# GpSimd's splits cut into tiles, a new order at the end of the activation, and routing sums as accumulating products

## The chip, the cores and the metric

The kernel runs on one core of one Trainium2 chip. The metric is the device time of the whole kernel in microseconds (us), as the median of several executions. TensorE does the matrix products (PE in the profile; PEld is its load of the stationary operand), VectorE (DVE), ScalarE (ACT) and GpSimd (POOL) the elementwise work, and SyncE (SP) issues the DMA transfers. SBUF is the on-chip memory, PSUM the accumulators that TensorE writes.

## What is computed

Linear attention by random features, a dense layer with the mish activation, and a mixture of experts with one expert per token, cut from the reference:

```python
# q, k, v: 2 x 8 heads x 576 x 64; omega: 128 x 64
def phi(x):
    proj = einsum('bhsd,md->bhsm', x, omega); sq = sum(x*x)/2
    h = proj - sq
    return exp(h - max(h)) / sqrt(m)
kv = einsum('bhsm,bhsd->bhmd', phi(k), v); z = sum(phi(k), axis=2)
x = num / den            # num = phi(q) kv,  den = phi(q) z + 1e-6
...
h = x @ w_in             # 1152 tokens x 512 -> 2048
g = h * tanh(softplus(h))
y = g @ w_out            # 2048 -> 512
...
logits = y @ w_gate      # 8 experts
e = argmax(logits); gate = softmax(logits)[e]
# in token order: a token is kept while its expert has fewer than `capacity` (288) tokens
out = gate * (relu(y @ w1[e]) @ w2[e])   # 0 for tokens that are not kept
```

## The kernel before

**Precision.** Large operands are float32 and are split into a high part in fp32r (a rounded copy) and a low part (what the rounding left): `split_hi_lo`, one cast (L56 on ScalarE, L58 on GpSimd, L60 on VectorE) and one subtraction (L62, on VectorE or GpSimd). Each product is then three matmuls (L66, L67, L68), so every operand is split before TensorE can start on it. `w_in` and `w_out` arrive as words that VectorE first turns into float32, in three instructions to a chunk (L109, L111, L113).

**Attention (0 to about 80 us).** The 16 heads are taken in 8 pairs `p`, in a loop over `i`; a pass of it has five beats, each with one `proj` on TensorE (`pj`), one `phi` (the maximum on VectorE, the exponential on ScalarE, for some halves after a subtraction on VectorE, L235), and extra work for earlier pairs: transposes (`qtr`, result `qT`), sums over keys (`kvm`), `den` and `num` (L282). The operand `kqf` of a pair (1024 columns for an even one, 1280 for an odd one) is loaded two or three passes ahead, by a DMA on SyncE's queue whose buffer must have been released by an earlier split, and split into `kqh` and `kql`: by ScalarE and VectorE for pair 0, ScalarE and GpSimd for pair 1, and GpSimd alone for pairs 2 to 7, in one cast and one subtraction for the whole pair, issued before the first beat of a pass. `num` ends with a split of its own result `x` (576 columns) into `xh` and `xl` on GpSimd. VectorE converts the first chunks of `w_in` in between. The order of each engine's instructions in this stage is the order of the code.

**h (about 80 to 200 us).** For 16 blocks `j` of the hidden layer and 3 groups `c` of tokens, `hmm(j,c)` is a product of `x` and `w_in`, and `hout` copies it to `g` (L422). `mish` turns `g` into the activation in steps: "s" (sigmoid) and "l" (logarithm) on ScalarE, "t" a tanh on ScalarE (L470) and a product on VectorE (L471). ScalarE has to load a table (`table`) between kinds of function. `wturn` and `wgate_u`/`wgate_s` work out w_out · w_gate, so that the logits (`lg`, L477) come from `g` itself; `wgate_s` waits for a copy `us` of `wgate_u`'s result (L441).

**First pass over w_out (about 202 to 245 us).** `ymm(ps0,j)` adds block `j` of `g` times `w_out` for a first group of 288 tokens; `prep(j)` splits `w_out`'s block (`wl`, `whi`) and `g`'s (`gh`) ahead of it. Between the 16 products stand the last logits and the routing: `route0` (argmax, as a one-hot `oh`), `route1` (each token's place among the tokens of its expert, `rp`), `route2` (counts, and which expert's tokens take the next steps). From here on everything is an order written by hand. Then come a second pass for a group of tokens that the routing chose, two experts, and a rest that is skipped when no token is left.

In `route1`, a token's place is the sum over earlier tokens in its tile (a product with `ub`, a triangle of ones) and over all earlier tiles: the latter from `cu`, a running sum of the one-hots over the 12 tiles of 96 tokens, made in `route0` by copies and additions on VectorE (L660 to L666):

```python
T.matmul(out=p[:TT, 0:96], lhsT=ub, rhs=fl(R["ohb"]), start=True, stop=False)
T.matmul(out=p[:TT, 0:96], lhsT=onesb, rhs=fl(R["cu"]), start=False, stop=True)
```

Of the kernel before, what the change touches and what calls it, by code (L numbers as in the profile page):

```python
# [32 lines left out]
def performer_mish_moe(  # L33
# [132 lines left out]
    with ExitStack() as c2:  # L166
# [136 lines left out]
        def num(u, k, last=False):  # L303
# [13 lines left out]
            split_hi_lo(x, xh[:, e + k, c], xl[:, e + k, c], *(("act", "dve") if last else ("pool", "pool")))  # L317
# [98 lines left out]
    with tc.manual_schedule():  # L416
# [19 lines left out]
        def wgate_u(b):  # L436
# [4 lines left out]
            S.copy(out=us[b], in_=u)  # L441
# [37 lines left out]
        chunk, ghl = {}, {}  # L479

# [31 lines left out]
        for j in range(NJ):  # L512
# [20 lines left out]
            for c in range(3):  # L533
                if (j, c) not in h_early:
                    hout(j, c, hmm(j, c))
                if c == 0:
# [27 lines left out]
                if c == 1:  # L564
# [3 lines left out]
                    if j == 15:  # L568
                        prep(1, slice(0, GT), "dve", "pool")
# [14 lines left out]
        prep(2, slice(0, GT), "dve", "pool")  # L584
# [22 lines left out]
        def route0(lgs):  # L607
# [25 lines left out]
            V.tensor_scalar(out=cand, in0=pv, scalar1=0.0, scalar2=-1000.0, op0=ALU.is_ge, op1=ALU.mult)  # L633
            yield
            V.tensor_tensor(out=cand, in0=cand, in1=iota, op=ALU.add)
            yield
# [12 lines left out]
            V.tensor_reduce(out=sm, in_=ex, op=ALU.add, axis=AX.X)
# [6 lines left out]
            R["gate"] = gate  # L656
            cu = [small(f"cu{i}", sh, BF16) for i in range(2)]
            V.memset(cu[0][:, 0:1, :], 0.0)
            yield
            V.tensor_copy(out=cu[0][:, 1:, :], in_=ohb[:, 0 : NTT - 1, :])  # L660
            yield
            k, a = 1, 0
            while k < NTT:
                V.tensor_copy(out=cu[1 - a][:, 0:k, :], in_=cu[a][:, 0:k, :])
                yield
                V.tensor_tensor(out=cu[1 - a][:, k:, :], in0=cu[a][:, k:, :], in1=cu[a][:, : NTT - k, :], op=ALU.add)  # L666
                yield
                k, a = 2 * k, 1 - a
            R["ohb"], R["cu"] = ohb, cu[a]

        def route1():
            fl = lambda a: a.rearrange("p t e -> p (t e)")
            sh = [TT, NTT, E]
            p = bank("qt", "rp")
            T.matmul(out=p[:TT, 0:96], lhsT=ub, rhs=fl(R["ohb"]), start=True, stop=False)
# [324 lines left out]
```

## Time and profile before

| | |
|---|---|
| time, median of 3 runs | 333.21 us (332.83 to 333.98) |
| the profiled execution | 333.5 us, of it 331.7 us the span that the trace covers |
| mean granted clock of TensorE | 0.975 |
| busy, share of the span | PE 93%, PEld 84%, DVE 67%, ACT 61%, POOL 26% |
| the chain that ended last | PE 73%, DVE 11%, ACT 7%, DMA 4% |

The span is from the first to the last instruction on the trace; the rest of the profiled time lies around it. The granted clock is TensorE's share of full speed. The busy share is an average over stages: what a change in one of them is worth has to be read from that stage's own waits.

### The profile page before, as it was taken

To read this page: it belongs to the slowest core of one execution; us is meant where nothing else is said; L and a number is where in the kernel's file an instruction comes from. 1 tells how busy PE (TensorE), PEld (TensorE's weight loads), DVE (VectorE), ACT (ScalarE), POOL (GpSimd) and SP (SyncE) were. 2 spreads that over 40 slices of the span, in tenths; PEclk is the share of its full clock that TensorE was granted. 3 is DMA by queue.
4 is the path that set the end of the run, shared out by engine and by line. 5 is a ranking of instruction groups with operands and counts; after the bars stand their busy time and mean duration, and the time that the engine had idled before them with its cause. 6 is when DMAs were issued, how large, how long until landed. Compare 5 with 4: busy or idle time off the path is not lost.

```text
span 331.7 us, 5881 instructions
## 1 busy us (share of the span) xinstructions
PE 307.7 (93%) x2223; PEld 279.4 (84%) x2224; DVE 221.6 (67%) x405; ACT 201.2 (61%) x383; POOL 85.1 (26%) x65
## 2 busy tenths in 40 slices
PE   8978988999999999999999998499599999999992
PEld 5966865877999899889988995489599999999991
DVE  5769897763798696977778489498564465314411
ACT  5955674765149978878797795745244672506311
POOL 2884682213000000000000013477401460332300
PEclk9997997999999999999999999899799999999998
DMA  7796532000066339926160000000034545441011
GB/s 216 248 322 204 176 104 87 28 0 2 0 204 241 128 127 300 278 89 218 38 251 2 0 2 0 0 4 1 2 109 138 166 127 191 158 131 54 21 36 41
DMA packets 18065, 36.88 MB, mean 111 GB/s; under 512 B 1552, under 2 KB 7376, under 8 KB 18032
## 3 DMA queue, kind: packets, MB, share of 16 engines
q1 hardware_dynamic: 18032, 36.45, 33.7%
q8 instruction: 19, 0.31, 0.4%
q14 instruction: 14, 0.11, 0.1%
HBM read 32.91 MB, written 3.54 MB: 110 GB/s over the span
## 4 chain that ended last, share of the span: by engine, by line
PE 73%; DVE 11%; ACT 7%; DMA 4%; issue 2%; SPq 1%; POOL 1%; ACTq 0%; POOLq 0%; DVEq 0%
PE h L66 9%; PE h L67 9%; PE h L68 9%; PE py L66 7%; PE py L67 7%; PE py L68 7%; PE kvp L249 3%; PE num L282 3%; PE ph L66 2%; PE ph L67 2%; PE ph L68 2%; DMA wi<-w_in 2%; DVE wif L113 2%; PE lg L477 2%; PE wt L433 2%
## 5 line engine op out<-in xcount | busy, mean ns | idle before, releaser
L62 POOL TENSOR_TENSOR wl<-wl,whi 128x512 fp32r<-128x512 f32 x32 | 44.2, 1384 | 191.6 <-DVE whi L60 131.1
L66 PE MATMUL h<-xh,wih 128*128 128x384 f32 x192 | 66.5, 346 | 0.5 <-DVE g L422 0.5
L68 PE MATMUL h<-xh,wil 128*128 128x384 f32 x192 | 64.4, 336 | 0.0
L67 PE MATMUL h<-xl,wih 128*128 128x384 f32 x192 | 64.4, 336 | 0.0
L66 PE MATMUL py<-gh,whi 128*128 128x288 f32 x128 | 39.8, 311 | 1.3 <-DVE g L422 1.3
L66 PEld LDWEIGHTS h<-xh,wih 128*128 128x128 f32 x192 | 36.1, 188 | 5.0 <-issue 2.9
L68 PE MATMUL py<-gh,wl 128*128 128x288 f32 x128 | 39.2, 307 | 0.0
L67 PE MATMUL py<-gh,whi 128*128 128x288 f32 x128 | 39.1, 305 | 0.0
L67 PEld LDWEIGHTS h<-xl,wih 128*128 128x128 f32 x192 | 36.1, 188 | 0.5 <-issue 0.5
L68 PEld LDWEIGHTS h<-xh,wil 128*128 128x128 f32 x192 | 36.0, 188 | 0.0
L471 DVE TENSOR_TENSOR g<-g,em 128x1152 f32<-128x1152 f32 x16 | 22.7, 1426 | 13.9 <-ACT em L470 13.9
L230 DVE TENSOR_REDUCE nm<-pj 128x4 f32<-128x512 f32 x36 | 24.3, 686 | 11.4 <-PE pj L68 11.2
L237 ACT ACTIVATE e<-pj,nm 128x128 f32<-128x128 f32 x72 | 22.4, 382 | 15.3 <-DVE e L235 8.5
L66 PEld LDWEIGHTS py<-gh,whi 128*128 128x128 f32 x128 | 25.4, 199 | 6.7 <-issue 3.7
L62 DVE TENSOR_TENSOR gh<-g,gh 128x288 fp32r<-128x288 f32 x32 | 21.4, 672 | 12.1 <-ACT gh L56 11.8
L56 ACT CAST gh<-g 128x288 fp32r (+1 forms) x26 | 11.3, 434 | 25.7 <-PE py L68 21.3
L68 PEld LDWEIGHTS py<-gh,wl 128*128 128x128 f32 x128 | 25.4, 199 | 0.0
L67 PEld LDWEIGHTS py<-gh,whi 128*128 128x128 f32 x128 | 25.4, 198 | 0.0
L56 ACT CAST whi<-wl 128x512 fp32r<-128x512 f32 x41 | 24.2, 616 | 1.1 <-PE py L67 1.0
L66 PE MATMUL pj<-omh,kqh 128*128 128x256 f32 x72 | 22.9, 319 | 0.8 <-ACT e L240 0.8
L422 DVE COPY g<-h 128x384 f32<-128x384 f32 x36 | 19.9, 552 | 4.2 <-PE h L68 4.2
L458 ACT ACT_TABLE_LOAD x17 | 21.8, 1283 | 0.3
(156 smaller groups left out, 735.0 us busy)
## 6 DMA issues: line engine op xcount, KB each, us to landing
wi<-w_in SPq DMA_DIRECT2D x16, 512.0 KB, 3.6
wo<-w_out SPq DMA_DIRECT2D x16, 512.0 KB, 4.7
wl<-w SPq DMA_DIRECT2D x32, 256.0 KB, 3.0
out<-zero SPq DMA_DIRECT2D x1, 2304.0 KB, 11.6
kqf<-kq SPq DMA_DIRECT2D x3, 640.0 KB, 4.0
v<-va SPq DMA_DIRECT2D x4, 390.0 KB, 4.4
kqf<-kq SPq DMA_DIRECT2D x3, 512.0 KB, 5.2
v<-va SPq DMA_DIRECT2D x4, 260.0 KB, 4.9
```

Of the source, the lines that this page charges most:

```text
L56: S.copy(out=hi, in_=src)
L62: e.tensor_tensor(out=lo, in0=src, in1=hi.bitcast(F32), op=ALU.subtract)
L66: T.matmul(out=o, lhsT=lh, rhs=rh, start=start, stop=False)
L67: T.matmul(out=o, lhsT=lh, rhs=rl, start=False, stop=False)
L68: T.matmul(out=o, lhsT=ll, rhs=rh, start=False, stop=stop)
L230: V.tensor_reduce(out=nm, in_=pv, op=ALU.max, axis=AX.X, negate=True)
L237: S.activation(out=e[:, j, :], in_=pv[:, j, :], func=AF.Exp, bias=nm[:, j : j + 1])
L249: T.matmul(out=K[:, c : c + 65], lhsT=e[t][:, h, :], rhs=v[:, (2 * t + h) * 65 : (2 * t + h + 1) * 65], start=(p % 2 == 0 and h == 0 and t ...
L282: T.matmul(out=o[32 * i : 32 * i + 32, :GT], lhsT=d[w][:, h, r, s], rhs=d["qT"][:, r, h, c * GT : c * GT + GT], start=True, stop=True, til ...
L422: (S.copy if c == 2 and j < 12 else V.tensor_copy)(out=g(j, slice(c * 384, c * 384 + 384)), in_=ps)
L458: nc.scalar.preload_act_table_set(name)
L471: V.tensor_tensor(out=hv, in0=hv, in1=em.pop(j), op=ALU.mult)
```

## The change

Three parts.

1. **Attention.** The splits of pairs 2 to 7 are cut into pieces of 256 columns, of which one is issued before each beat; the split of `x` in `num` is cut in two.
2. **End of the activation and first pass.** `prep(0)` moves from block 15 to the end of block 14; the tanh of block 13 is taken apart from its product ("ta", "tp"); blocks 2 to 5 of `w_out` get their low part on VectorE, later ones on GpSimd as before; the last copy `us` goes to VectorE; the `prep`s stand three products ahead at first; the logits come after product 4 (before: 5), `route0` after 5 (before: 6), `route1` after 8 (before: 10).
3. **Routing.** The running sums are 11 more products with ones, each over the first 96 − 8k columns, accumulated in the same place as the product with `ub`; the one-hot is made in bf16 at once; gate values and the rest that isn't needed for the choice of experts come later.

```diff
-            return (("act", "dve"),) * 3 if p == 0 else (("act", "pool"),) * 2 if p == 1 else (("pool", "pool"),)
+            return (("act", "dve"),) * 3 if p == 0 else (("act", "pool"),) * 2 if p == 1 else (("pool", "pool"),) * 5
...
-            for c, e in zip(pieces(p), halves(p)):
+            cut = pieces(p) if p < 2 else [slice(c, c + 256) for c in range(0, 1280 if p % 2 else 1024, 256)]
+            for c, e in zip(cut, halves(p)):
...
+                for i in range(2):
+                    s = slice(i * GT, i * GT + GT)
+                    t = slice(b * SEQ + i * GT, b * SEQ + i * GT + GT)
+                    split_hi_lo(x[:, s], xh[:, e + k, t], xl[:, e + k, t], "pool", "pool")
...
-            if i + 2 < NPAIR and i > 0:
-                finish(split(i + 2))
+            sp = split(i + 2) if i + 2 < NPAIR and i > 0 else iter(())
+            advance(sp)
             beat(i, 0, *([lambda: den(u) if odd else num(u, 1)] if u >= 0 else []))
...
+                advance(sp)
                 beat(i, t + 1, *extra[t])
+            finish(sp)
...
-            S.copy(out=us[b], in_=u)
+            (V.tensor_copy if b == 3 else S.copy)(out=us[b], in_=u)
...
                     elif j == 15:
-                        prep(0, slice(0, GT), "dve", "pool")
                         mish("t", 12)
                         mish("s", 14)
-                        mish("t", 13)
+                        mish("ta", 13)
...
+                        prep(0, all0, "dve", "pool")
...
-        prep(2, slice(0, GT), "dve", "pool")
+        mish("tp", 13)
+        prep(2, all0, "dve", "dve")
...
-            ohb = small("ohb", sh, BF16)
-            V.tensor_copy(out=ohb, in_=oh)
...
-            V.tensor_copy(out=cu[0][:, 1:, :], in_=ohb[:, 0 : NTT - 1, :])
-            yield
-            k, a = 1, 0
-            while k < NTT:
-                V.tensor_copy(out=cu[1 - a][:, 0:k, :], in_=cu[a][:, 0:k, :])
-                yield
-                V.tensor_tensor(out=cu[1 - a][:, k:, :], in0=cu[a][:, k:, :], in1=cu[a][:, : NTT - k, :], op=ALU.add)
-                yield
-                k, a = 2 * k, 1 - a
...
-            T.matmul(out=p[:TT, 0:96], lhsT=onesb, rhs=fl(R["cu"]), start=False, stop=True)
+            for k in range(1, NTT):
+                T.matmul(out=p[:TT, k * E : 96], lhsT=onesb, rhs=fl(R["oh"])[:, 0 : 96 - k * E], start=False, stop=(k == NTT - 1))
...
         for j in range(NJ):
-            if j == 1:
-                wo_split(3, "dve", "pool")
-            if j + 2 < NJ and j > 0:
-                g_split(j + 2, all0, "dve" if j < 4 else "act", "dve")
-            if j + 3 < NJ and j > 0:
-                wo_split(j + 3, "dve" if j < 4 else "act", "pool")
+            if j == 2:
+                mish("t", 14)
+                mish("t", 15)
+            if j + 2 < NJ and j > 3:
+                prep(j + 2, all0, "act", "pool")
             advance(*[chain] * pace)
             ymm(ps0, j)
-            if j == 1:
+            if j < 3:
+                prep(j + 3, all0, "act" if j == 2 else "dve", "dve")
+            if j == 2:
                 wgate_s(3)
-            if j == 3:
-                mish("t", 14, 15)
-            if j == 5:
+            if j == 4:
                 logits(3)
...
-            if j == 6:
-                chain, pace = route0(lgs), 7
+            if j == 5:
+                finish(route0(lgs))
+            if j == 8:
+                route1()
+            if j == 9:
+                chain, pace = route2(), 6
                 advance(chain)
             if j == 10:
-                advance(*[chain] * 40)
-                route1()
-            if j == 12:
-                chain, pace = route2(), 7
-                advance(chain)
+                finish(gates())
```

**What moves: GpSimd in the attention stage.** GpSimd's instructions for the splits of pairs 3, 4 and 5 before (`kqh` the high, `kql` the low part; the number behind a name counts tiles):

```order
L58 TENSOR_SCALAR kqh_209<-kqf_205 128x1280
L62 TENSOR_TENSOR kql_210<-kqf_205,kqh_209 128x1280
L58 TENSOR_SCALAR kqh_307<-kqf_303 128x1024
L62 TENSOR_TENSOR kql_308<-kqf_303,kqh_307 128x1024
L58 TENSOR_SCALAR kqh_403<-kqf_395 128x1280
L62 TENSOR_TENSOR kql_404<-kqf_395,kqh_403 128x1280
```

and now, from the last piece of pair 3 to the first pieces of pair 5 ("x2" is two in a row):

```order
L58 TENSOR_SCALAR kqh_215<-kqf_211 128x256
L58 TENSOR_SCALAR kqh_321<-kqf_317 128x256
L62 TENSOR_TENSOR kql_216<-kqf_211,kqh_215 128x256
L62 TENSOR_TENSOR kql_322<-kqf_317,kqh_321 128x256
L58 TENSOR_SCALAR kqh_321<-kqf_317 128x256 x2
L62 TENSOR_TENSOR kql_322<-kqf_317,kqh_321 128x256 x2
L58 TENSOR_SCALAR kqh_321<-kqf_317 128x256
L62 TENSOR_TENSOR kql_322<-kqf_317,kqh_321 128x256
L58 TENSOR_SCALAR kqh_423<-kqf_415 128x256 x2
L62 TENSOR_TENSOR kql_424<-kqf_415,kqh_423 128x256 x2
```

One instruction has become four or five, in the same total of columns; the pieces of one pair stand close together, and the last of a pair is mixed with the first of the next. The orders of TensorE, VectorE, ScalarE and SyncE in this stage are the same before and after.

**What moves: VectorE at the end of the activation.** VectorE's instructions around the last copies of block 15 before (`g7` holds blocks 14 and 15, `g6` blocks 12 and 13, `g0` blocks 0 and 1; `em` is the tanh):

```order
L422 COPY g7_1183<-h_2254 128x384
L60 CAST whi_2268<-wl_1200 128x512
L60 CAST gh_2272<-g0_1176 128x288
L62 TENSOR_TENSOR gh_2272<-g0_1176,gh_2272 128x288
L471 TENSOR_TENSOR g6_1182<-g6_1182,em_2185 128x1152
L471 TENSOR_TENSOR g6_1182<-g6_1182,em_2203 128x1152
L422 COPY g7_1183<-h_2281 128x384
L60 CAST whi_2301<-wl_1210 128x512
L60 CAST gh_2305<-g0_1176 128x288
L62 TENSOR_TENSOR gh_2305<-g0_1176,gh_2305 128x288
L422 COPY g7_1183<-h_2308 128x384
```

and now:

```order
L60 CAST whi_2308<-wl_1254 128x512
L60 CAST gh_2312<-g0_1230 128x288
L62 TENSOR_TENSOR gh_2312<-g0_1230,gh_2312 128x288
L431 COPY g7_1237<-h_2315 128x384
L481 TENSOR_TENSOR g6_1236<-g6_1236,em_2239 128x1152
L431 COPY g7_1237<-h_2334 128x384
L60 CAST whi_2354<-wl_1264 128x512
L60 CAST gh_2358<-g0_1230 128x288
L62 TENSOR_TENSOR gh_2358<-g0_1230,gh_2358 128x288
L431 COPY g7_1237<-h_2361 128x384
L481 TENSOR_TENSOR g6_1236<-g6_1236,em_2257 128x1152
```

The three instructions of `prep(0)` stand ahead of block 15's first copy instead of behind it, and the second product of `g6` stands behind the last copy instead of ahead of the second.

**What moves: TensorE at the routing.** TensorE's instructions at the routing's places before, behind the last matmul of product 10:

```order
L68 MATMUL py_2360<-gh_2577,wl_2542 128x288
L675 LDWEIGHTS ub_61
L675 MATMUL rp_2657<-ohb_2588,ub_61 96x96
L676 LDWEIGHTS onesb_62
L676 MATMUL rp_2657<-cu0_2595,onesb_62 96x96
```

and now, behind the last of product 8 (the first three of twelve):

```order
L68 MATMUL py_2414<-gh_2596,wl_2593 128x288
L655 LDWEIGHTS ub_61
L655 MATMUL rp_2649<-oh_2590,ub_61 96x96
L657 LDWEIGHTS onesb_62
L657 MATMUL rp_2649<-oh_2590,onesb_62 96x88
L657 LDWEIGHTS onesb_62
L657 MATMUL rp_2649<-oh_2590,onesb_62 96x80
```

No product reads `cu` any more; all read the one-hot `oh`.

## Rows read from the trace of the kernel before

**Rows 1.** The profile's page: the line of TensorE's granted clock over 40 slices of the span (in tenths of full speed), and GpSimd's costliest group (count | busy us, mean ns | idle before).

```profile
PEclk9997997999999999999999999899799999999998
...
L62 POOL TENSOR_TENSOR wl<-wl,whi 128x512 fp32r<-128x512 f32 x32 | 44.2, 1384 | 191.6 <-DVE whi L60 131.1
```

**Rows 2.** TensorE's timeline (start us, length us, engine, line, operation, tiles, and in brackets the idle time before it with what ended that): the longest waits before the second pass over w_out, and the logits (`lg`).

```profile
25.27 1.19 PE L282 MATMUL den<-qT,z 128*32 128x288 f32 x8 [2.26 <-ACT qT L275]
...
30.95 0.38 PE L66 MATMUL pj<-omh,kqh 128*128 128x256 f32 x1 [0.79 <-ACT e L240]
...
51.22 0.69 PE L282 MATMUL num<-qT,kv 128*32 128x288 f32 x8 [2.59 <-DVE t L299]
...
204.99 0.40 PE L66 MATMUL py<-gh,whi 128*128 128x288 f32 x1 [1.33 <-DVE g L422]
...
211.86 0.66 PE L447 MATMUL ws<-cs,us 128*128 128x128 f32 x4 [4.23 <-ACT us L441]
...
222.43 0.40 PE L66 MATMUL py<-gh,whi 128*128 128x288 f32 x1
...
235.66 0.20 PE L676 MATMUL rp<-cu,onesb 96*96 96x96 bf16 x1 [3.59 <-DVE cu L666]
```

**Rows 3.** Stretches of the span, with the busy time of each engine, the granted clock of TensorE (PEclk), the DMA share and GB/s.

```profile
25.30:28.30 3.00, 3.00 (x17) 2.08 (x18) 2.97 (x2) 0.31 (x1) 3.00 (x1) 0.50 0.83 279
52.50:56.00 3.50, 3.50 (x22) 2.36 (x20) 2.26 (x6) 2.33 (x8) 1.07 (x2) 0.52 0.00 0
205.10:207.60 2.50, 2.50 (x18) 2.30 (x18) 2.46 (x6) 2.47 (x3) 1.31 (x2) 1.00 0.00 0
212.80:216.10 3.30, 3.30 (x16) 3.30 (x16) 2.07 (x7) 1.12 (x2) 1.27 (x1) 0.51 0.00 0
236.80:240.20 3.40, 3.40 (x16) 3.40 (x15) 0.65 (x2) 0.96 (x2) 1.04 (x1) 0.51 0.02 5
240.20:245.20 5.00, 5.00 (x39) 4.99 (x39) 2.76 (x19) 2.09 (x6) 0.24 (x1) 1.00 0.06 12
```

**Rows 4.** VectorE's timeline in the attention stage: the conversion of w_in (`wif`), three instructions to a chunk.

```profile
22.21 1.74 DVE L109 TENSOR_SCALAR wif<-wi 128x512 int32<-128x512 int32 x1 [2.01 <-DMA wi<-w_in]
...
24.20 1.49 DVE L111 SCALAR_TENSOR_TENSOR wif<-wi,wif 128x512 int32<-128x512 int32 x1
25.73 3.33 DVE L113 SCALAR_TENSOR_TENSOR wif<-wi,wif 128x512 int32<-128x512 int32 x1
...
43.15 1.32 DVE L109 TENSOR_SCALAR wif<-wi 128x512 int32<-128x512 int32 x1
44.50 1.63 DVE L111 SCALAR_TENSOR_TENSOR wif<-wi,wif 128x512 int32<-128x512 int32 x1
...
46.66 2.84 DVE L113 SCALAR_TENSOR_TENSOR wif<-wi,wif 128x512 int32<-128x512 int32 x1
```

**Rows 5.** GpSimd's timeline in the attention stage: the high parts (L58) and low parts (L62) of the splits.

```profile
7.26 1.29 POOL L62 TENSOR_TENSOR kql<-kqf,kqh 128x512 fp32r<-128x512 f32 x1 [5.82 <-ACT kqh L56]
...
16.57 2.96 POOL L62 TENSOR_TENSOR kql<-kqf,kqh 128x1280 fp32r<-128x1280 f32 x1
...
23.90 1.26 POOL L58 TENSOR_SCALAR kqh<-kqf 128x1280 fp32r<-128x1280 f32 x1 [0.23 <-DMA kqf<-kq]
25.24 3.26 POOL L62 TENSOR_TENSOR kql<-kqf,kqh 128x1280 fp32r<-128x1280 f32 x1
...
45.68 3.27 POOL L62 TENSOR_TENSOR kql<-kqf,kqh 128x1280 fp32r<-128x1280 f32 x1
54.84 0.67 POOL L58 TENSOR_SCALAR xh<-xf 128x576 fp32r<-128x576 f32 x1 [5.89 <-DVE xf L315]
```

**Rows 6.** VectorE's groups by line and shape from 85 to 190 us, where GpSimd has no instruction (line, engine, operation, tiles, count | busy us, mean ns | idle before).

```profile
L62 DVE TENSOR_TENSOR wil<-wif,wih 128x512 fp32r<-128x512 f32 x13 | 9.0, 691 | 5.5 <-ACT wih L56 5.0
...
L113 DVE SCALAR_TENSOR_TENSOR wif<-wi,wif 128x512 int32<-128x512 int32 x13 | 8.9, 683 | 0.0
...
L109 DVE TENSOR_SCALAR wif<-wi 128x512 int32<-128x512 int32 x13 | 5.4, 419 | 0.0
```

**Rows 7.** The waits of SyncE's DMA queue from 0 to 90 us (us in total, times, longest us).

```profile
SPq L195 <- POOL kql L62: 15.6, 5, 4.0
```

**Rows 8.** The chain that ended last, from 10 to 60 us: the first load of w_in.

```profile
15.46 6.73 DMA wi<-w_in
```

**Rows 9.** VectorE's timeline at the end of the activation and in the routing.

```profile
200.64 1.36 DVE L471 TENSOR_TENSOR g<-g,em 128x1152 f32<-128x1152 f32 x1 [0.75 <-ACT em L470]
...
203.05 1.41 DVE L62 TENSOR_TENSOR gh<-g,gh 128x288 fp32r<-128x288 f32 x1
...
213.10 0.46 DVE L62 TENSOR_TENSOR gh<-g,gh 128x288 fp32r<-128x288 f32 x1
...
231.89 1.25 DVE L660 COPY cu<-ohb 96x88 bf16<-96x88 bf16 x1
```

**Rows 10.** ScalarE's timeline at the end of the activation.

```profile
205.03 1.17 ACT L466 ACTIVATE em<-g 128x1152 f32<-128x1152 f32 x1 [3.94 <-DVE g L422]
...
211.22 0.59 ACT L441 COPY us<-wu 128x512 f32<-128x512 f32 x1
211.71 2.22 ACT L470 ACTIVATE em<-em 128x1152 f32<-128x1152 f32 x2
```

**Rows 11.** The weight loads of TensorE (PEld) at the routing's product.

```profile
231.74 0.12 PEld L675 LDWEIGHTS <-ub 96*96 96x96 bf16 x1
```

More of the change, by code (lines that the diff above doesn't have):

```diff
@@ L479, in performer_mish_moe @@
         chunk, ghl = {}, {}
+        all0 = slice(0, GT)
         def ring_tiles(k):
@@ L624, in route0, with route1, gates @@
             V.tensor_reduce(out=mx, in_=pv, op=ALU.max, axis=AX.X)
-            yield
             V.tensor_tensor(out=pv, in0=pv, in1=bc(mx), op=ALU.subtract)
-            yield
             ex = small("ex", sh)
             S.activation(out=ex, in_=pv, func=AF.Exp)
-            yield
             cand = small("cand", sh)
[L633 to L636, printed above, removed]
+            V.scalar_tensor_tensor(out=cand, in0=pv, scalar=0.0, in1=iota, op0=ALU.is_ge, op1=ALU.mult)
             idx = small("idx", [TT, NTT])
             V.tensor_reduce(out=idx, in_=cand, op=ALU.min, axis=AX.X)
-            yield
-            oh = small("oh", sh)
+            oh = small("oh", sh, BF16)
             V.tensor_tensor(out=oh, in0=cand, in1=bc(idx), op=ALU.is_equal)
-            yield
-            R["oh"] = oh
-            ohb = small("ohb", sh, BF16)
-            V.tensor_copy(out=ohb, in_=oh)
-            yield
+            R["oh"], R["ex"] = oh, ex
+        def route1():
+            fl = lambda a: a.rearrange("p t e -> p (t e)")
+            sh = [TT, NTT, E]
+            p = bank("qt", "rp")
+            T.matmul(out=p[:TT, 0:96], lhsT=ub, rhs=fl(R["oh"]), start=True, stop=False)
+            for k in range(1, NTT):
+                T.matmul(out=p[:TT, k * E : 96], lhsT=onesb, rhs=fl(R["oh"])[:, 0 : 96 - k * E], start=False, stop=(k == NTT - 1))
+            kb = small("kb", sh, BF16)
+            V.scalar_tensor_tensor(out=fl(kb), in0=p[:TT, 0:96], scalar=capf[:, 0:1], in1=fl(R["oh"]), op0=ALU.is_lt, op1=ALU.mult)
+            R["kb"] = kb
+        def gates():
+            sh = [TT, NTT, E]
             sm = small("sm", [TT, NTT])
-            V.tensor_reduce(out=sm, in_=ex, op=ALU.add, axis=AX.X)
+            V.tensor_reduce(out=sm, in_=R["ex"], op=ALU.add, axis=AX.X)
             yield
@@ L655, in route0 @@
             yield
-            R["gate"] = gate
-            cu = [small(f"cu{i}", sh, BF16) for i in range(2)]
-            V.memset(cu[0][:, 0:1, :], 0.0)
+            wt = cpool.tile(sh, F32, name="wt")
+            V.tensor_tensor(out=wt, in0=R["kb"], in1=gate[:, :, None].to_broadcast(sh), op=ALU.mult)
+            R["wt"] = wt
             yield
-            V.tensor_copy(out=cu[0][:, 1:, :], in_=ohb[:, 0 : NTT - 1, :])
-            yield
-            k, a = 1, 0
-            while k < NTT:
-                V.tensor_copy(out=cu[1 - a][:, 0:k, :], in_=cu[a][:, 0:k, :])
-                yield
-                V.tensor_tensor(out=cu[1 - a][:, k:, :], in0=cu[a][:, k:, :], in1=cu[a][:, : NTT - k, :], op=ALU.add)
-                yield
-                k, a = 2 * k, 1 - a
[L669 to L675, printed above, removed]
-            T.matmul(out=p[:TT, 0:96], lhsT=onesb, rhs=fl(R["cu"]), start=False, stop=True)
-            kp = small("kp", sh)
-            V.scalar_tensor_tensor(out=fl(kp), in0=p[:TT, 0:96], scalar=capf[:, 0:1], in1=fl(R["oh"]), op0=ALU.is_lt, op1=ALU.mult)
-            kb = small("kb", sh, BF16)
-            V.tensor_copy(out=kb, in_=kp)
-            R["kb"] = kb
-            wt = cpool.tile(sh, F32, name="wt")
-            V.tensor_tensor(out=wt, in0=kp, in1=R["gate"][:, :, None].to_broadcast(sh), op=ALU.mult)
-            R["wt"] = wt
         def route2():
@@ L715, in route2 @@
             yield
-            rem = small("rem", [1, 1])
-            V.tensor_reduce(out=rem, in_=cnt, op=ALU.add, axis=AX.X)
-            yield
-            V.tensor_tensor(out=rem, in0=rem, in1=m0[:, 0:1], op=ALU.subtract)
-            yield
-            V.tensor_tensor(out=ri[:, 3:4], in0=rem, in1=m1[:, 0:1], op=ALU.subtract)
-            yield
-            cnti = cpool.tile([1, G * E], I32, name="cnti")
-            V.tensor_copy(out=cnti, in_=cnt)
-            yield
-            R["cnti"], R["ri"] = cnti, ri
+            R["ri"] = ri
             ET = mybir.EngineType
@@ L737, in route2 @@
             R["wA"], R["wB"] = wA, wB
+            rem = small("rem", [1, 1])
+            V.tensor_reduce(out=rem, in_=cnt, op=ALU.add, axis=AX.X)
+            yield
+            V.tensor_tensor(out=rem, in0=rem, in1=m0[:, 0:1], op=ALU.subtract)
+            yield
+            V.tensor_tensor(out=ri[:, 3:4], in0=rem, in1=m1[:, 0:1], op=ALU.subtract)
+            yield
+            cnti = cpool.tile([1, G * E], I32, name="cnti")
+            V.tensor_copy(out=cnti, in_=cnt)
+            R["cnti"] = cnti
         def expert_load(e, n, c):
```

12 lines of the change are left out of this document (7 added, 5 removed).

## The prediction

> **What bounds the kernel now.** I start from the granted clock over the span: TensorE is at full clock but for dips in the first quarter and around two thirds of the span [rows 1]. TensorE's timeline tells what precedes them. Between the start and the second pass over w_out it waits longest for the transposes' copy (2.26 us, at 25.27), a product of the attention's end (2.59, at 51.22), the copy `us` (4.23, at 211.86) and the running sums `cu` (3.59, at 235.66) [rows 2]. The stretches behind these four are at 0.50 to 0.52 of the clock, its level of 1.2 GHz; behind the 1.33 us wait that ends at 204.99 the clock stayed at 1.00, 2.4 GHz [rows 3]. Each fall lasted 3.0 to 3.5 us, so it cost about half of that, 1.5 to 1.7 us, beside the wait itself. The four waits and falls are 12.7 + 6.5 = 19.2 us; in between TensorE has work without a pause, so what is saved there lands in the time almost one for one.
>
> Why VectorE is late in the attention is in its own timeline. The conversion of a chunk takes 0.42, 0.68 and 0.68 us where GpSimd does nothing [rows 6]. In the attention the same three took 1.74, 1.49 and 3.33, later 1.32, 1.63 and 2.84 [rows 4]. Set beside GpSimd's timeline, the 3.33 us instruction ended 0.56 after GpSimd's 3.26 us subtraction (25.24 to 28.50), and the 2.84 us one 0.55 after that of 45.68 to 48.95 [rows 5]: an undisturbed run begun when GpSimd ended. So two such instructions from SBUF exclude each other for a whole instruction, and what VectorE waits depends on how long GpSimd's instruction is.
>
> **Attention: pieces.** A subtraction takes 1.29 us for 512 columns and 2.96 for 1280, a cast 0.67 for 576 and 1.26 for 1280 [rows 5]: 2.17 and 0.84 ns a column, so by extension 0.73 and 0.40 for 256. A pair of 1280 columns takes 5 × 1.13 = 5.65 instead of 4.2, one of 1024 some 4.5 instead of 3.5; GpSimd is idle most of the span, so this costs only where somebody waits for a split's end. One does: SyncE's next load of `kqf`, which waits for a split (five times, 15.6 us) [rows 7], and behind it in the same queue the first chunk of w_in, issued at 15.46 and 6.73 on its way [rows 8]. VectorE waits for just that chunk at 22.21. The split that releases it becomes up to 1.0 later; some of that the transfers take up, and I take 0.5.
>
> *First wait (25.27).* It ends with a copy that follows VectorE's first conversion (22.21), since the subtraction for `e` stands behind it. Of 1.74 us, 1.32 is waiting; with pieces a wait is at most 0.73 and I take 0.45. So 0.9 less, 0.5 later: 0.4 gained, the gap is 1.85. That lies between the 1.33 without and the 2.26 with a fall; I let the fall stand. VectorE's next two waited 0.81 and 2.65, of which some 2.5 goes; it was late for TensorE's wait at 30.95, 0.79 us [rows 2], which goes. Together 1.2 (0.3 with the load a full 1.0 late and half the later gap left; 2.9 with no fall).
>
> *Second wait (51.22).* In VectorE's stretch before it three instructions waited 0.9 + 0.95 + 2.16 = 4.0 us [rows 4]. GpSimd's pieces now last longer and meet five or so of VectorE's instructions at 0.3 to 0.7; I take 2.05, so VectorE is 1.95 earlier and the gap is 0.6, well under 1.33, without a fall: 1.95 + 1.6 = 3.5 (0.5 if the pieces meet all five at 0.7, 4.2 if they meet three at 0.45). The split `x` costs GpSimd 0.3 more each, where it idles for microseconds before the next. Attention: 4.7.
>
> **End of the activation.** The last copy of block 15 releases ScalarE's sigmoid at 205.03, for which ScalarE had idled 3.94 us [rows 10]. Ahead of it VectorE waited 0.75 and worked 1.36 on a product at 200.64 [rows 9], now behind it: 2.1 earlier, so 202.9. The copy `us` (0.59 at 211.22 [rows 10]) leaves ScalarE, so the pair of tanh starts at 209.0 instead of 211.71 and ends at 211.2. TensorE meanwhile: five products of 12 matmuls, at 39 in 5.00 us [rows 3] 1.54 each, from about 202.6, and 0.4 of transposes: 210.7. VectorE prepares a block with two casts and two subtractions (0.69 [rows 6] and 0.46 [rows 9]) in some 1.6 to 1.9 and keeps just behind, 211.3. The 4.23 us wait goes, but the next one takes its place: the last logits need both products of 14 and 15 on VectorE (1.36 each; the second from 211.4 to 212.8), then two low parts and a sum (0.69 + 0.46 + 0.28), behind which GpSimd's low part of block 6, 1.38 us [rows 1], stands in the way. VectorE's low part of `gh` at 203.05 took 1.41 so, against 0.46 at 213.10 [rows 9]; I add 1.1. Logits start at 215.3, a gap of 4.0, so a fall as before. Logits 2.07 (220.36 to 222.43 [rows 2]), product 5 1.54, fall 1.65: 220.6, where before the same six products and the logits were done at 222.43. 1.8 gained (0.8 if the sigmoid gains only 1.1; 3.1 without GpSimd's turn).
>
> **Routing.** TensorE's wait of 3.59 for `cu` goes: VectorE's copies and sums (the first 1.25 long, at 231.89 [rows 9]) stood there. With it goes the fall behind it (236.80 to 240.20 at 0.51 [rows 3]): 1.65. What comes are 11 products of at most 88 columns, each with a load of the ones. A load of 96 columns took 0.12 [rows 11], a small product 0.20 in its record [rows 2]; if only the load counts, 1.3, if both, 3.5. I take 1.3, as TensorE's matmuls overlap their loads everywhere in these rows. So 3.59 + 1.65 − 1.3 = 3.94 (1.7 to 5.2). The Trainium skill, TensorE: Matmul & The Clock Gate, section LDWEIGHTS, gives a load as the columns over 1.2, in ns: by it 0.08 each, 0.9 in all, and a sum 0.4 better; the row's 0.12 decides. The gate values, off this chain, are VectorE's work beside later products and cost nothing as long as it idles there. From the second pass on, nothing changes but its start.
>
> **Sum.** 1.2 + 3.5 + 1.8 + 3.94 = 10.4. The profiled execution took 333.5, 0.3 over the median of 333.21: 333.5 − 10.4 = **323.0**.
>
> **Rivals.**
> *Attention gains nothing.* The waits move: the later load and the longer splits eat what shorter instructions give; the sum of GpSimd's time rises, so VectorE may meet it more often. For it: splits 30% longer, SyncE's queue behind them. Against: 2.65 and 2.16 us of waiting for single subtractions. 333.5 − 5.7 = 327.8.
> *The gaps that I left also close.* The first attention gap stays without a fall (1.7) and GpSimd's block 6 falls elsewhere (1.3): 320.0.
> *The end is worth little.* 0.8 for the activation; the 11 products cost load and matmul, 3.5. Speaking for it: the order puts the low part of block 8's `gh` behind the whole of `route0` on VectorE, seven small instructions of which one can take 1.25 where GpSimd is in the way, so a wait before product 8 may replace that for `cu`. 4.7 + 0.8 + 1.7 = 7.2: 326.3.
> *Slower: short pieces leave VectorE no opening.* If GpSimd begins its next instruction before VectorE can, VectorE waits for a whole run of pieces: at 22.21 for pairs 4 and 5 together, from about 20.1 for 4.5 + 5.65 to 30.3, instead of 23.95, which costs TensorE some 5.5 after later waits that vanish; in the second stretch from 43.15 to about 51, 6.5 later less 3.1 of waits it then no longer has, 3.5. 333.5 + 9 − 5.7 = 337; it decides from an attention loss of 5.7 on. Against it: VectorE's instruction at 24.20 did get in between GpSimd's cast (to 25.16) and subtraction (from 25.24, 0.3 longer than the 2.96 of its kind) [rows 4, 5]. The Trainium skill, GPSIMD Engine Reference, section 2.1 on instruction dispatch, says that consecutive instructions there are no barrier and that a core starts the next as soon as it has done its share, which would leave no opening; the rows at 24.20 and 25.24 speak against that here.
>
> **Chances.** Forecast 0.50, attention nothing 0.20, the gaps close 0.12, the end is worth little 0.12, slower 0.06. The range 318.5 to 328.5 takes in the first four with their rounding and leaves the slower case out; the likeliest one's own is 321 to 325.5. About 0.3%, 1 us, is what a measurement of this kernel can tell from no change: faster by more 0.92, within 0.03, slower 0.05.
>
> **What would show it.** In the trace after: VectorE's conversions in the attention each under 1.5 us; the wait at 51 under 1 us with a clock of 1.00 behind it; TensorE idle about 4 us once between products 4 and 5, ended by VectorE's sum for the gate, and nowhere at the routing, where twelve short products take 1.5 us; the second pass begins near 235. Wrong it would be if a conversion waits over 2 us beside pieces, if TensorE waits over 2 us for `oh` or for a `gh` behind it, or if the products take 0.3 each.

## The result and the profile after

The changed kernel takes 324.73 us in the median of 4 runs (323.91 to 325.63), the kernel before 333.6 (332.83 to 334.57): a ratio of 0.9733, 95% interval 0.9691 to 0.9775, or about 8.9 us less. The profiled execution took 324.12, with a span of 322.3 where the kernel before had 331.7, and a mean granted clock of 0.986 (before 0.975). The ratio and interval of every run compare only the faster executions of both kernels, while the medians printed beside them are of all, so a ratio below can lie nearer to 1 than its two medians.

TensorE's timeline after in the attention, in the form of [rows 2]. Line numbers of the changed kernel are up to some 20 higher or lower.

```profile
26.57 1.19 PE L283 MATMUL den<-qT,z 128*32 128x288 f32 x8 [2.90 <-ACT qT L276]
...
32.05 0.69 PE L283 MATMUL num<-qT,kv 128*32 128x288 f32 x8
...
48.80 0.69 PE L283 MATMUL num<-qT,kv 128*32 128x288 f32 x8 [0.34 <-DVE t L300]
```

The same from 190 us on: the logits of block group 2 (the first `lg` row; h is done there), the last logits (the second), the transposes of `route0`, and the twelve products of the routing:

```profile
195.70 2.14 PE L487 MATMUL lg<-g,wg 128*32 128x384 f32 x24
...
211.31 3.48 PE L487 MATMUL lg<-g,wg 128*32 128x384 f32 x24 [3.25 <-DVE wg L457]
...
216.44 1.47 PE L626 MATMUL rp<-cs,lgs 128*96 128x128 f32 x12
...
223.01 0.21 PE L655 MATMUL rp<-oh,ub 96*96 96x96 bf16 x1
223.06 0.62 PE L657 MATMUL rp<-oh,onesb 96*96 96x88 bf16 x11
```

The first matmul behind these in the same timeline:

```profile
223.54 0.38 PE L66 MATMUL py<-gh,whi 128*128 128x288 f32 x1
```

and the longest wait in the rest of the pass:

```profile
232.58 0.40 PE L67 MATMUL py<-gh,whi 128*128 128x288 f32 x1 [0.61 <-DVE gh L62]
```

Set beside [rows 2], the wait for `cu` (3.59) is gone, the one for `us` (4.23) has become one of 3.25 for the gate's sum (L457), the second of the attention (2.59) is down to 0.34, and the first (2.26) has *grown* to 2.90. The stretch behind the first of these, in the form of [rows 3]:

```profile
26.60:30.00 3.40, 3.40 (x20) 2.48 (x21) 3.06 (x6) 3.00 (x9) 3.40 (x6) 0.54 0.83 243
```

and those behind the second, behind the wait for the sum, and at the routing:

```profile
48.80:52.00 3.20, 3.20 (x32) 2.11 (x33) 3.20 (x7) 2.46 (x8) 3.20 (x6) 1.00 0.24 96
211.30:214.70 3.40, 3.39 (x24) 0.99 (x24) 0.86 (x2) 0.48 (x1) 0.00 (x0) 0.59 0.02 5
...
222.00:236.00 14.00, 13.38 (x108) 13.13 (x107) 11.40 (x33) 6.53 (x16) 8.91 (x7) 1.00 0.18 58
```

The clock fell behind the first wait (0.54) and behind the one for the sum (0.59), and no longer behind the second of the attention or at the routing (1.00).

Where the 9.4 us between the two profiled spans came from can be read off from four places that both kernels pass. The rows of the kernel before that [rows 2] lacks are its logits of group 2 and its first wait in the experts:

```profile
199.66 2.14 PE L477 MATMUL lg<-g,wg 128*32 128x384 f32 x24
...
276.16 0.40 PE L66 MATMUL ph<-yt,whi 128*128 128x288 f32 x1 [0.32 <-DVE h L761]
```

and the latter in the changed kernel:

```profile
266.44 0.40 PE L66 MATMUL ph<-yt,whi 128*128 128x288 f32 x1 [0.34 <-DVE h L752]
```

The logits of group 2 start at 195.70, at 199.66 before: attention, 3.96. From there to the point at which six products and all logits are done, it is 20.74 (216.44) against 22.77 ([rows 2]: 222.43 less 199.66): end of the activation, 2.03. From there to TensorE's first wait in the experts (266.44 after, 276.16 before) 50.00 against 53.73: routing, 3.73. From there to the end 55.86 against 55.54: 0.32 lost.

### The profile page after: what moved, and what is told of

Its sections match the earlier page's. It is cut to its first block, busy times and chain, and to the rows that moved or that the text cites. A ratio compares the mean times of both kernels' runs of the same rounds, so it can differ in the third digit from the quotient of the medians.

```text
span 322.3 us, 5943 instructions
## 1 busy us (share of the span) xinstructions
PE 305.6 (95%) x2233; PEld 276.6 (86%) x2234; DVE 216.1 (67%) x394; ACT 202.2 (63%) x385; POOL 89.8 (28%) x115
## 4 chain that ended last, share of the span: by engine, by line
PE 73%; DVE 11%; ACT 7%; DMA 3%; issue 3%; SPq 1%; POOL 0%; DVEq 0%; ACTq 0%; POOLq 0%
PE h L66 9%; PE h L67 9%; PE h L68 9%; PE py L67 5%; PE py L68 5%; PE py L66 5%; PE kvp L250 3%; DVE gh L62 3%; PE num L283 3%; PE lg L487 2%; PE ph L66 2%; PE ph L67 2%; PE ph L68 2%; PE pj L66 2%; PE pj L68 2%
## 5 line engine op out<-in xcount | busy, mean ns | idle before, releaser
L62 POOL TENSOR_TENSOR wl<-wl,whi 128x512 fp32r<-128x512 f32 x28 | 37.6, 1351 | 192.5 <-ACT em L477 117.8
L67 PE MATMUL py<-gh,whi 128*128 128x288 f32 x128 | 38.2, 299 | 0.9 <-DVE gh L62 0.8
L66 PE MATMUL py<-gh,whi 128*128 128x288 f32 x128 | 38.4, 300 | 0.0
L68 PE MATMUL py<-gh,wl 128*128 128x288 f32 x128 | 37.7, 294 | 0.0
L62 DVE TENSOR_TENSOR gh<-g,gh 128x288 fp32r<-128x288 f32 x32 | 22.5, 712 | 13.8 <-ACT gh L56 13.7
L481 DVE TENSOR_TENSOR g<-g,em 128x1152 f32<-128x1152 f32 x16 | 21.6, 1357 | 13.4 <-ACT em L479 13.3
L56 ACT CAST whi<-wl 128x512 fp32r<-128x512 f32 x43 | 25.4, 616 | 2.1 <-DVE sm L668 1.1
L67 PEld LDWEIGHTS py<-gh,whi 128*128 128x128 f32 x128 | 24.2, 189 | 1.8 <-DVE gh L62 1.8
L66 PEld LDWEIGHTS py<-gh,whi 128*128 128x128 f32 x128 | 24.0, 188 | 1.6 <-DVE gh L62 0.8
L62 POOL TENSOR_TENSOR kql<-kqf,kqh 128x256 fp32r<-128x256 f32 (+2 forms) x29 | 23.3, 824 | 7.3 <-ACT kqh L56 7.1
L68 PEld LDWEIGHTS py<-gh,wl 128*128 128x128 f32 x128 | 24.1, 189 | 0.0
L62 DVE TENSOR_TENSOR wl<-wl,whi 128x512 fp32r<-128x512 f32 x20 | 16.9, 845 | 8.6 <-PE py L68 3.6
```

The source lines that it names most:

```text
L56: S.copy(out=hi, in_=src)
L62: e.tensor_tensor(out=lo, in0=src, in1=hi.bitcast(F32), op=ALU.subtract)
L66: T.matmul(out=o, lhsT=lh, rhs=rh, start=start, stop=False)
L67: T.matmul(out=o, lhsT=lh, rhs=rl, start=False, stop=False)
L68: T.matmul(out=o, lhsT=ll, rhs=rh, start=False, stop=stop)
```

## The experiments

The interval with each is that of its ratio to the kernel before on the same chip.

**Each part by itself.** First the attention's pieces in the kernel before:

```diff
...
-            for c, e in zip(pieces(p), halves(p)):
+            cut = pieces(p) if p < 2 else [slice(c, c + 256) for c in range(0, 1280 if p % 2 else 1024, 256)]
+            for c, e in zip(cut, halves(p)):
...
+            sp = split(i + 2) if i + 2 < NPAIR and i > 0 else iter(())
+            advance(sp)
...
```

> The kernel before with the first part of the change alone: splits of pairs 2 to 7 in pieces of 256 columns, x in two halves. All other engines keep their order. My account of the two traces (h's end at 199.66 before, at 195.70 after) gives this part 4.0 us, all of it from the second wait (51.22: about 2.3 of waiting and 1.6 of the fall behind it) and next to none from the first (25.27), which stays about 2.9 us long with its fall: 329.6 where the kernel before takes 333.6. Rival: the parts need each other (the attention's gain is lost in the end of the activation, which waits for other engines): within 1 us of before.

329.75 us against 334.16, ratio 0.9911 (0.9869 to 0.9953): about 3.0 us, with an interval of 1.6 to 4.4 that takes in the 4.0 expected and leaves out the rival. The part stands alone. One thing differs from the changed kernel, in TensorE's timeline of this kernel: the first wait was 3.09 us long, and the clock did not fall behind it (den 0.69 long, and 1.00 in the window):

```profile
26.31 0.69 PE L283 MATMUL den<-qT,z 128*32 128x288 f32 x8 [3.09 <-ACT qT L276]
```

Its window, in the form of [rows 3]:

```profile
26.30:29.80 3.50, 3.49 (x33) 3.02 (x34) 3.41 (x7) 3.15 (x9) 3.50 (x6) 1.00 0.91 292
```

Then the routing in the kernel before, with `gates` after `route1`. The part also makes `cand`, an operand of the argmax, in one instruction of VectorE instead of two, here and in the changed kernel:

```diff
...
-            T.matmul(out=p[:TT, 0:96], lhsT=onesb, rhs=fl(R["cu"]), start=False, stop=True)
+            for k in range(1, NTT):
+                T.matmul(out=p[:TT, k * E : 96], lhsT=onesb, rhs=fl(R["oh"])[:, 0 : 96 - k * E], start=False, stop=(k == NTT - 1))
...
+            if j == 11:
+                finish(gates())
...
```

> The kernel before with the third part alone: running sums as 11 accumulating products with ones, one-hot in bf16 at once, gate values after the choice; products, logits and routing steps stay where they were among the 16 products. Theory: the wait for cu (3.59) and the fall behind it (1.65) go, the 11 products cost 0.5 as in the trace after: 4.7 less, 328.9, with the stretch behind the products at a clock of 1.00. Rival: the one-hot takes the place of cu as what is late, since VectorE's small instructions wait for GpSimd's low parts of w_out (1.3 each): a wait of 1 to 2 us before the products and a gain of 2 to 3.5.

328.32 us against 334.16, 0.9848 (0.9787 to 0.991), and in the trace there is no wait at the products and the clock behind them is full. TensorE's timeline of this kernel has the eleven products (the second row) within 0.62 us:

```profile
233.01 0.21 PE L644 MATMUL rp<-oh,ub 96*96 96x96 bf16 x1
233.05 0.62 PE L646 MATMUL rp<-oh,onesb 96*96 96x88 bf16 x11
```

The window behind them:

```profile
235.00:238.50 3.50, 3.50 (x28) 3.49 (x28) 2.67 (x10) 1.39 (x3) 1.87 (x2) 1.00 0.02 5
```

Then the second and third part without the first:

```diff
...
-            cut = pieces(p) if p < 2 else [slice(c, c + 256) for c in range(0, 1280 if p % 2 else 1024, 256)]
-            for c, e in zip(cut, halves(p)):
+            for c, e in zip(pieces(p), halves(p)):
...
```

> The changed kernel with the attention as before the change: splits of whole pairs, x in one. The second and third part alone. By the traces they gave 2.0 (end of the activation) and 3.7 (routing) up to the second pass, less 0.3 at the end: 5.5 under the kernel before, a ratio of 0.984. Routing alone gave 0.985, so the end of the activation would add next to nothing over it if the rival holds (the 3.25 us wait for the sum, with its fall, takes what the earlier sigmoid gave), and 2.0 (0.979) if both add in full.

328.58 us against 335.17, 0.988 (0.981 to 0.9951). That is the routing alone once more (0.9848) within both intervals. The 0.979 that the two parts would give if both added in full lies just outside this run's interval, but it is built on the routing's ratio, which is itself uncertain by 0.006. The trace has the 2.0 us:

```profile
198.40 2.14 PE L479 MATMUL lg<-g,wg 128*32 128x384 f32 x24
...
219.25 1.47 PE L618 MATMUL rp<-cs,lgs 128*96 128x128 f32 x12
```

From the logits of group 2 (198.40) to the transposes of `route0` (219.25) it is 20.85, against 20.74 in the changed kernel and 22.77 before. So the end of the activation is seen in the trace and not in the times, whose intervals are 4 to 5 us wide; which of the two the many executions bear out stays open. Multiplied, the ratios of the attention (0.9911) and of the other two parts (0.988) give 0.979 where the whole change has 0.9733; the intervals allow for either. The remaining wait of this run, in TensorE's timeline, is the same as after:

```profile
213.98 3.64 PE L479 MATMUL lg<-g,wg 128*32 128x384 f32 x24 [3.22 <-DVE wg L449]
```

**The wait for the sum.** In the changed kernel, VectorE's timeline has these as its last instructions before the logits:

```profile
206.40 2.63 DVE L481 TENSOR_TENSOR g<-g,em 128x1152 f32<-128x1152 f32 x2
208.94 1.75 DVE L62 TENSOR_TENSOR wl<-wl,whi 128x512 fp32r<-128x512 f32 x1
210.61 0.45 DVE L62 TENSOR_TENSOR gh<-g,gh 128x288 fp32r<-128x288 f32 x1
210.98 0.28 DVE L457 TENSOR_REDUCE wg<-ws 128x32 f32<-128x128 f32 x1
```

and GpSimd's has the low part of block 6 next to them:

```profile
208.85 1.29 POOL L62 TENSOR_TENSOR wl<-wl,whi 128x512 fp32r<-128x512 f32 x1 [10.74 <-ACT whi L56]
```

The sum (L457) stands behind two low parts, of which the first took 1.75 instead of its undisturbed 0.69 [rows 6], since GpSimd had begun 0.09 earlier. The experiment puts the sum first:

```diff
+            if j == 2:
+                wgate_s(3)
             if j < 3:
                 prep(j + 3, all0, "act" if j == 2 else "dve", "dve")
-            if j == 2:
-                wgate_s(3)
```

> The changed kernel with one exchange: the sum over w_gate's part (VectorE, ended the 3.25 us wait before the last logits) stands ahead of the two low parts of block 5 instead of behind them. Theory: the logits wait for two low parts of 1.75 and 0.45, of which 1.06 was GpSimd's turn; without them they start 2.2 earlier, the gap is about 1.1, and the clock does not fall behind it (1.4 more): 321 where the changed kernel takes 324.7. Rival: the wait moves to product 5, whose low parts are now later, and the clock falls there: 323 to 324.

321.06 us against 334.16, 0.9609 (0.9535 to 0.9683). In TensorE's timeline the gap is 1.18, and product 5 does not wait:

```profile
207.79 2.14 PE L487 MATMUL lg<-g,wg 128*32 128x384 f32 x24 [1.18 <-DVE wg L457]
```

The clock behind it is full:

```profile
207.70:211.20 3.50, 3.41 (x34) 2.02 (x35) 2.72 (x5) 1.68 (x4) 1.09 (x2) 1.00 0.02 5
```

**Why the first wait grew.** VectorE's conversions of w_in in the changed kernel, in the form of [rows 4]:

```profile
22.28 2.98 DVE L109 TENSOR_SCALAR wif<-wi 128x512 int32<-128x512 int32 x1 [1.41 <-DMA wi<-w_in]
...
25.51 0.87 DVE L111 SCALAR_TENSOR_TENSOR wif<-wi,wif 128x512 int32<-128x512 int32 x1
26.42 0.77 DVE L113 SCALAR_TENSOR_TENSOR wif<-wi,wif 128x512 int32<-128x512 int32 x1
...
43.99 1.17 DVE L111 SCALAR_TENSOR_TENSOR wif<-wi,wif 128x512 int32<-128x512 int32 x1
...
45.69 1.20 DVE L113 SCALAR_TENSOR_TENSOR wif<-wi,wif 128x512 int32<-128x512 int32 x1
```

GpSimd's timeline beside the first of them:

```profile
22.43 0.80 POOL L58 TENSOR_SCALAR kqh<-kqf 128x256 fp32r<-128x256 f32 x2
23.17 1.44 POOL L62 TENSOR_TENSOR kql<-kqf,kqh 128x256 fp32r<-128x256 f32 x2
24.55 0.43 POOL L58 TENSOR_SCALAR kqh<-kqf 128x256 fp32r<-128x256 f32 x1
25.06 0.77 POOL L62 TENSOR_TENSOR kql<-kqf,kqh 128x256 fp32r<-128x256 f32 x1
```

All but one are short, as forecast. The first waited 2.56 us, through two high and two low pieces (22.43 to 24.61) and a third high one, and got in at about 24.98, where GpSimd paused for 0.08 before the low piece of that same high one. In [rows 5] the pause after 23.90 + 1.26 = 25.16, before the low part at 25.24, is the same, and there the conversion at 24.20 got in. Between high, high, low and low there is no such pause: each row begins some 0.06 before the one before it ends. That order isn't the code's: a scheduler orders the attention stage, contrary to what is said of that stage ahead of the prediction, and moves a second high piece in ahead of the first low one. In the next experiments pieces overlap by 8 columns, which are written twice with the same values, so that each high piece must come after the low piece before it; all other engines keep their order.

```diff
...
+            w = 1280 if p % 2 else 1024
+            o = 8 if p > 4 else 0
+            cut = pieces(p) if p < 2 else [slice(max(c - o, 0), c + 256) for c in range(0, w, 256)]
```

> The changed kernel, where the pieces of pairs 4 to 7 overlap by 8 columns, so that GpSimd must take them in the order high, low, high, low instead of high, high, low, low; all other engines keep their order. Theory: GpSimd lets VectorE in only where it waits for its own result (a low part right behind its own high part, 0.08 us of a pause in the trace); in the order high, high, low, low nothing waits, and VectorE's conversion at 22.28 waited 2.56 us through two of each. By turns it waits for one or two pieces, 1.2 at most, so its length is under 1.7, the gap before den 1.3 shorter than 2.90 and the time 1 to 2.7 lower than the changed kernel's 324.7, 322 to 323.7. Rival: only the length of an instruction counts, or chance: the conversion waits as long, 324.7 within 0.5.

The text says pairs 4 to 7, but the edit (`p > 4`) begins with pair 5, and the conversion at 22.28 meets pair 4. Ratio 0.9756 (0.9694 to 0.9817), as the changed kernel: the later pairs' order is worth nothing that can be told. Only times are read of this run, not its trace. With `p > 3`:

> The changed kernel with the overlap of 8 columns from pair 4 on, so that GpSimd takes high and low pieces by turns where VectorE's first conversion meets it (the run before left out pair 4). Other engines keep their order. In three traces with the order high, high, low, low (after, attention alone, sum first) that conversion took 2.98, 2.71 and 2.99 us and came in each time right behind the first high piece with its own low piece next. Theory (GpSimd lets VectorE in only where it waits for its own result): it now takes 0.4 to 1.5, the conversion's 1.2 at most of waiting, and the gap before den falls from 2.8 to 3.1 to about 1.6; 1 to 1.3 us less than the changed kernel's 324.7, so about 323.5, or 2.5 less where the fall behind the gap was. Rival (length of the pieces alone, or chance): the conversion takes 2.5 to 3 again.

VectorE's timeline of this kernel, the same conversion:

```profile
22.05 0.43 DVE L110 TENSOR_SCALAR wif<-wi 128x512 int32<-128x512 int32 x1 [1.93 <-DMA wi<-w_in]
...
22.72 0.68 DVE L112 SCALAR_TENSOR_TENSOR wif<-wi,wif 128x512 int32<-128x512 int32 x1
23.44 1.12 DVE L114 SCALAR_TENSOR_TENSOR wif<-wi,wif 128x512 int32<-128x512 int32 x1
```

GpSimd's beside it:

```profile
22.10 0.65 POOL L59 TENSOR_SCALAR kqh<-kqf 128x264 fp32r<-128x264 f32 x1
22.83 1.18 POOL L63 TENSOR_TENSOR kql<-kqf,kqh 128x264 fp32r<-128x264 f32 x1
24.09 0.74 POOL L59 TENSOR_SCALAR kqh<-kqf 128x264 fp32r<-128x264 f32 x1
```

and TensorE's wait for den:

```profile
23.79 0.69 PE L286 MATMUL den<-qT,z 128*32 128x288 f32 x8 [0.87 <-ACT qT L279]
```

320.45 us against 335.32, ratio 0.9553 (0.9505 to 0.9601), an interval that lies below that of the changed kernel. The conversion took 0.43, the next 0.68 and 1.12, and the gap before den is 0.87. GpSimd's pieces are longer than alone (1.18 for a low one of 264 columns): now it is GpSimd that waits. The logits of group 2 start at 191.67, 4.0 before the changed kernel's 195.70; 1.6 of that is the fall that the latter's trace has behind den, the rest, 2.4, is more than the 1.0 to 1.3 expected, since the gap is smaller by 2.0, and the wait at 48.80 (0.34) is gone too.

So the order by turns took the long wait away, in this trace and in that of the sum first by turns below. It does not show the theory behind it, that GpSimd lets VectorE in *only* at a pause: other rows speak against that. In the changed kernel, VectorE's low part of the same chunk

```profile
27.87 0.82 DVE L62 TENSOR_TENSOR wil<-wif,wih 128x512 fp32r<-128x512 f32 x1
```

met two low pieces of GpSimd, which don't need each other and have no pause between them:

```profile
27.42 1.87 POOL L62 TENSOR_TENSOR kql<-kqf,kqh 128x256 fp32r<-128x256 f32 x2
```

It waited only 0.13 (0.69 alone [rows 6]) and got in between the two: the pair took 1.87, where such pairs took 1.44 at 23.17. In the last run below (the sum first, with whole splits up to pair 4), a conversion of the very kind that waited 2.56 did the same, 0.69 long where it takes 0.42 alone:

```profile
28.07 0.69 DVE L110 TENSOR_SCALAR wif<-wi 128x512 int32<-128x512 int32 x1 [0.41 <-DMA wi<-w_in]
```

and GpSimd's pair around it took 1.64:

```profile
27.72 1.64 POOL L63 TENSOR_TENSOR kql<-kqf,kqh 128x256 fp32r<-128x256 f32 x2
```

So behind a piece with no pause VectorE gets in as well. Why the first conversion alone was passed over at the ends of several pieces, in each of the three traces with that order (2.98, 2.71 and 2.99 long), and not elsewhere, stays open.

The first wait can also be had back by leaving the splits up to pair 4 whole, as before the change.

```diff
-            cut = pieces(p) if p < 2 else [slice(c, c + 256) for c in range(0, 1280 if p % 2 else 1024, 256)]
+            w = 1280 if p % 2 else 1024
+            cut = pieces(p) if p < 5 else [slice(c, c + 256) for c in range(0, w, 256)]
```

> The changed kernel with the splits of pairs 2 to 4 whole, as before the change; those of 5 to 7 in pieces. Other engines keep their order. If the first wait got longer by the pieces (longer by a third, and without openings), it goes back: the first load of w_in is issued near 15.5 instead of 16.9, VectorE's first conversion takes 1.3 to 1.8 and the gap before den is 1.7 to 2.3 instead of 2.8 to 3.1; the later conversions meet pair 5's pieces and stay under 1.3. Time 0.5 to 1.3 under the changed kernel's 324.7. Rival: the first wait comes from the load alone, whose landing does not move: gap and time as in the changed kernel.

323.69 us, 0.966 (0.9625 to 0.9696), an interval that overlaps that of the changed kernel at its edge. In VectorE's timeline the conversion took 1.73:

```profile
21.90 1.73 DVE L110 TENSOR_SCALAR wif<-wi 128x512 int32<-128x512 int32 x1 [1.45 <-DMA wi<-w_in]
```

in TensorE's the gap was 1.70:

```profile
24.95 0.69 PE L285 MATMUL den<-qT,z 128*32 128x288 f32 x8 [1.70 <-ACT qT L278]
```

and the window behind it shows a fall in this execution, twice as long as those of [rows 3]:

```profile
25.70:32.40 6.70, 6.70 (x36) 6.07 (x36) 4.80 (x11) 4.49 (x15) 5.53 (x9) 0.50 0.39 127
```

Conversion and gap are as expected here; by turns the gap came out below the 1.6 expected. By turns is the better of the two, but of the 4.1 us between the two traces (their logits of group 2 start at 191.67 and 195.78) some 3.3 is the price of this fall, half its length, and the smaller gap gives only 0.8.

**Together.** The sum first with each of the two:

> Sum first and pieces by turns from pair 4 on, together. Theory: both gains add: 321.1 less 1 to 1.3, about 320. Rival: pieces by turns give nothing: 321.

317.04 us (316.64 to 319.48) against 335.32, ratio 0.9479 (0.9435 to 0.9524): the fastest version here, some 2.6% below the changed kernel by the two ratios. Its ratio lies below that of the sum first alone (0.9535 to 0.9683), and below that of the turns alone with intervals that overlap at the edge (0.9505 to 0.9601); the time is below the 320 expected. VectorE's timeline shows the conversion once more, begun 0.02 behind a high piece and 0.25 longer for it:

```profile
22.25 0.67 DVE L110 TENSOR_SCALAR wif<-wi 128x512 int32<-128x512 int32 x1 [1.52 <-DMA wi<-w_in]
```

> Sum first and whole splits up to pair 4, together. Theory: gains add, 321.1 less 0.5 to 1.3, about 320.2. Rival: 321.

318.97 us (about 320.2 expected), 0.9524 (0.948 to 0.9568). TensorE's timeline has a gap before den of 1.79, much as without the sum first (1.70):

```profile
25.34 0.69 PE L285 MATMUL den<-qT,z 128*32 128x288 f32 x8 [1.79 <-ACT qT L278]
```

but here no fall followed:

```profile
25.40:29.00 3.60, 3.60 (x34) 3.13 (x35) 3.10 (x6) 3.52 (x10) 2.02 (x4) 1.00 0.87 277
```

## Why the prediction was right, and where it was not

The time forecast was 323.0 from a sum of 10.4 (which gives 323.1); measured were 9.4 between the profiled executions, and a median of 324.73. The miss of 1.0 is that of the first term; the other errors, 0.3 and 0.2 too little against 0.2 and 0.3 too much, cancel by luck. By its terms:

**First wait, 1.2 forecast, 0.2 measured.** `num` starts at 32.05; TensorE's timeline of the kernel before has it at 32.22:

```profile
32.22 0.69 PE L282 MATMUL num<-qT,kv 128*32 128x288 f32 x8 [0.30 <-DVE t L299]
```

The step that failed is "with pieces a wait is at most 0.73": VectorE waited 2.56 at 22.28. The prediction had this case among its rivals (short pieces leave VectorE no opening), there for whole stretches, where it came true for one instruction, and set it aside on a row in which VectorE got in between two instructions of GpSimd [rows 4, 5]. That row was of a low part behind its own high part, which the order printed ahead of the prediction no longer has in every place: high, high, low, low. The Trainium skill, GPSIMD Engine Reference, section 2.1 on instruction dispatch, has it that consecutive instructions are no barrier between GpSimd's cores. The trace agrees for pieces that don't need each other (22.43 to 24.98 without a pause); behind a needed one it shows 0.08 of a pause. Pieces by turns, with such a pause at each turn, brought the conversion from 2.98 to 0.43; that the pause is the cause is not shown, as VectorE got in without one at 27.87. That the fall behind this wait stood, as forecast, says little: with waits of 3.09 and 2.79 at the same place none followed. The load, the other part of the term, was wrong as well, with little effect: that of w_in was issued 1.5 later than in [rows 8], at 16.94, and landed at the same time, 22.28 against 22.21.

**Second wait, 3.5 forecast, 3.8 measured** (3.96 less 0.2). Five waits of VectorE were forecast at some 0.4 each; the conversions at 43.99 and 45.69 waited 0.49 and 0.52, the gap is 0.34 instead of 0.6, and no fall came.

**End of the activation, 1.8 forecast, 2.03 in the trace.** Set back by the attention's 3.96, the sigmoid comes at 202.95 (202.9 forecast) and the tanh pair at 209.16 (209.0). GpSimd's turn in the low part of block 5 cost 1.06 (1.1). The gap, 3.25 instead of 4.0, was smaller as the products on VectorE ended at 209.03 + 3.96 = 212.99 (212.8), while TensorE's five products reached to 208.06 + 3.96 = 212.0 (211.3).

**Routing, 3.94 forecast, 3.73 measured.** The wait and the fall are gone. Eleven products took 0.5 us, not 1.3, nor the 0.9 that the prediction has beside it: from 223.06 to the next product's start at 223.54, 0.044 each. That gave 0.8, and low parts of `gh` that came late on VectorE took as much, in the manner of the rival on the order of `route0`: TensorE waited 0.17 at 221.43, for one begun behind the whole of `route0` and lengthened by GpSimd's turn, and 0.61 at 232.58, for one behind a small instruction of `route2` that GpSimd held up.

**End, 0 forecast, 0.32 lost,** not followed up.

What would have shown it wrong did show at one place, a conversion that waits over 2 us; the rest came as forecast: a wait of 0.34 at the second place with a clock of 1.00, one wait (3.25) between products 4 and 5 that ends with the sum, and the second pass from 235 on.

## What to carry to other kernels

When VectorE and GpSimd exclude each other, short instructions on GpSimd give VectorE more places to get in, and in these traces it mostly took the next one. At one place it waited 2.56 us through a run of pieces that don't need each other, and letting each need the one before ended that: look in the order for such runs and try it, but don't count on a rule, as elsewhere VectorE got in without a pause. What sets TensorE's wait is what stands last on the engine it waits for, so put a short instruction that TensorE needs ahead of long ones that it does not need yet; that gave 3 to 4 us here. And read an argument's counterexample for the case that it is from: one row where VectorE got in said nothing of a row order that did not exist yet.

## What the runs showed of the chip

Whether the clock falls behind a wait of 1.7 to 3.3 us isn't set by its length alone. Den's gap was followed by a fall at 2.90 (the changed kernel, 0.54) and at 1.70 (whole up to pair 4, 0.50), by none at 3.09 (attention alone), 2.79 (sum first) and 1.79 (the two together), 1.00 in each window. The prediction took the length as the cause; 2.26 [rows 2] and 1.33 were too few rows for that. Nor has a fall one price: that of the whole splits lasted 6.7 us, against 3.0 to 3.5 in [rows 3]. What decides it stays open. Executions of one program may differ in part by this: those of attention alone reached from 327.74 us (clock 0.983) to 332.41 (0.975). So where a longer wait, with a fall, becomes one like the 1.33 us of [rows 3] or the 1.18 of the sum first, behind which none was seen, the gain is more than the difference in length.
